# Two fixed places in a step for GpSimd's work on first products, the second behind a wait on VectorE's minimum of pairs

## The chip, the cores and the metric

The kernel runs on one core of a Trainium2 chip. The metric is device time in microseconds (us) of one execution. A core has five engines that run their own queues in order and meet through semaphores: TensorE (PE in the profile, its weight loads PEld), VectorE (DVE), ScalarE (ACT), GpSimd (POOL) and SyncE (SP), which here only starts DMAs.

## The reference

```python
# q, k, v: (8, 8, 576, 64) float32
scores = q @ k^T / 8
kth    = 32nd largest of each row of 576 scores
attn   = softmax(where(scores >= kth, scores, -1e9)) @ v
x      = attn, heads side by side             # (4608, 512)
h      = x @ w_in                             # (4608, 2048)
g      = h if h >= 1; 0 if h <= -1; else (h + 1)^2 / 4
out    = g @ w_out                            # (4608, 512)
```

## The kernel before, in words

**Attention** goes in 144 steps, each for a pair of heads and up to 128 queries. TensorE makes the scores (`sp`, L367), ScalarE scales and copies them to `s` (L368). VectorE finds the 32 largest of each row. It does so on two half-length lists: `more`, the larger of each pair of scores, and `less`, the smaller of each (`pairs`, L381, each a TENSOR_TENSOR with two inputs in SBUF). MAX8 gives eight largest, MATCH_REPLACE8 (L388) takes them out, and so on; a scan (L460) merges the lists into `kth`, and SCALAR_TENSOR_TENSOR (L467, one per head) multiplies the exponentials `e` by `s >= kth` and sums them to `z`. In the next step VectorE takes the reciprocal of `z` (L413), and GpSimd multiplies `e` by it: the *division*, two operations (L420), and a small difference `excess` behind it (L423). ScalarE copies the halves of the words of `e` (L497), and two DMAs bring them turned as `wT`, which TensorE multiplies by `v` (`po`, L514).

**The two products with weights** fill TensorE between these. Four steps complete one tile `xT` of 128 rows. `hidden` (L547) makes the first products of a *group* of two blocks of 128 hidden units, 8 groups per tile; `read` has ScalarE make two relus of it, `r` (L558) and `g` (L566). What is left to do on a group stands in `bound`, on GpSimd: a clip of `r` to 0..1 (L573), its square (L575) and the sum with `g` (L576). `final` (L588) multiplies `g` by `w_out` into `py`, four groups after `hidden`; ScalarE copies `py` to `y` (L594) for the DMA to the output.

**The order** of every engine is the order in which the Python loop calls the operations (`manual_schedule`). The loop goes over steps `m`, each in seven slots. In the part behind the conversion of the weights, slot 0 has VectorE's first operations on step m and the division of step m-1; slot 3 has the maximum of pairs (`more`) of step m+1, the minimum (`less`) of step m and the MAX8 behind them; slot 5 the MAX8 on `less`, the scan and the two products. Slot 2 of every even step has scores for two steps and two `po`, and up to three groups of first products that are read together behind these.

`read` puts its `bound` in the queue `bounds` with the slot's number. At a slot's end those that are more than two slots old are called, three operations together. `read` also empties the queue to one entry first, since `r` has two buffers, and `final` calls entries until its own group is whole. With one tile per four steps, the reads of a cycle come in slots 2 and 5 of its first step, 1 and 5 of the second, 3 of the third, 0, 5 and 6 of the fourth (4 in place of 5 in most cases from step 96 on). "Early", while weights are converted, and behind the last step, the queue is emptied at each slot's end.

Of the kernel before, what the change touches and what calls it, by code (L numbers as in the profile page):

```python
# [11 lines left out]
F32 = mybir.dt.float32  # L12
# [5 lines left out]
ALU = mybir.AluOpType  # L18
# [8 lines left out]
def kernel(  # L27
# [10 lines left out]
    nc = tc.nc  # L38
    B, H, S, D = q.shape
    NTOK, DM = out.shape  # L40
    DFF = moe_w_in.shape[1]
    P = 128
# [8 lines left out]
    SH = S // 2  # L51
# [4 lines left out]
    GROUP = 2  # L56
# [64 lines left out]
    def needed(f, second):  # L121

        return (f // n_in) * (NK + n_in * n_out) + NK + (n_out * (f % n_in + 1) if second else 0)
# [53 lines left out]
    def run(ctx, paired):  # L177
# [197 lines left out]

        def pairs(st, op, name, bufs):
            s = st["s"]
            st[name] = x = att.tile([P, 2, SH], F32, name=name, bufs=bufs)  # L380
            nc.vector.tensor_tensor(out=x, in0=s[:, :, 0:SH], in1=s[:, :, SH:S], op=op)  # L381

        def largest(st, r):
            return [partial(nc.vector.max, out=eight(st["tops"], i, r), in_=st["rest"][:, i, :]) for i in range(2)]
# [6 lines left out]
        def first_top(st, between=None):  # L391
            s, e = st["s"], st["e"]
            if paired:
                pairs(st, ALU.max, "more", 2)
            if between is not None and paired:
                pairs(between, ALU.min, "less", 1)
            st["rest"] = st["more"] if paired else s
            st["tops"] = tops = att.tile([P, 2 * TOP_K], F32, name="tops", bufs=3)
            nmax = att.tile([P, 2], F32, name="nmax")
            for x in largest(st, 0):  # L400
                x()  # L401
            nc.scalar.activation(nmax, tops[:, 0:2 * SPLIT:SPLIT], AF.Copy, scale=-1.0)
            for i in range(2):
                nc.scalar.activation(e[:, i, :], s[:, i, :], AF.Exp, bias=nmax[:, i:i + 1])  # L404
                yield
# [132 lines left out]
        def mlp(xT, rows, pool, last):  # L538
            gs, group, whole_g = {}, 1 if last else GROUP, set()
            py = []  # L540

            def hidden(x):
                ph = ps.tile([P, group, P], F32, name="ph", tag="ph", bufs=3)
                for i in range(group):
                    f = x * group + i
                    for kk in range(NK):
                        nc.tensor.matmul(ph[:, i], w_in[:, kk, f * P:(f + 1) * P], xT[:, kk],  # L547
                                         start=(kk == 0), stop=(kk == NK - 1))

                reads.append(partial(read, x, ph))  # L550
                if not holding:
                    issue_reads()

            def read(x, ph):
                while len(bounds) > 1:
                    bounds.popleft()[1]()
                r = pool.tile([P, GROUP, P], F32, name="r", bufs=2)[:, 0:group]
                nc.scalar.activation(r, ph, AF.Relu, bias=half, scale=0.5 * unit)  # L558
                gs[x] = g = pool.tile([P, GROUP, P], F32, name="g", bufs=2 * LAG)[:, 0:group]
                if last:  # L560
                    nc.scalar.activation(g, ph, AF.Relu, bias=minus_half, scale=0.5 * unit)
                    nc.vector.scalar_tensor_tensor(out=r, in0=r, scalar=1.0, in1=r, op0=ALU.min, op1=ALU.mult)
                    nc.vector.tensor_tensor(out=g, in0=r, in1=g, op=ALU.add)
                    whole_g.add(x)
                    return
                nc.scalar.activation(g, ph, AF.Relu, bias=minus, scale=unit)  # L566
                by_act = converted < n_pieces and x % 2
                if by_act:
                    nc.scalar.activation(r, r, AF.Square)
                bounds.append((slots_done, partial(bound, x, r, g, by_act)))  # L570

            def bound(x, r, g, by_act):
                nc.gpsimd.tensor_scalar(r, r, 1.0, 0.0, ALU.min, ALU.max)  # L573
                if not by_act:
                    nc.gpsimd.tensor_tensor(out=r, in0=r, in1=r, op=ALU.mult)  # L575
                nc.gpsimd.tensor_tensor(out=g, in0=r, in1=g, op=ALU.add)  # L576
                whole_g.add(x)

            def final(f):
                if f == 0:  # L580
                    while outputs:
                        outputs.popleft()[1]()
                    py.append(ps.tile([P, DM], F32, name="py", tag="py", bufs=1))
                if f // group not in gs:
                    issue_reads()
                while f // group not in whole_g:
                    bounds.popleft()[1]()
                nc.tensor.matmul(py[0], gs[f // group][:, f % group], w_out[:, f, :], start=(f == 0), stop=(f == NF - 1))  # L588
                if f == NF - 1:
                    outputs.append((slots_done, partial(give, py[0])))  # L590

            def give(total):
                y = (late or words).tile([P, DM], F32, name="y", bufs=1)
                nc.scalar.activation(y, total, AF.Copy, scale=unit)  # L594
                for p0, p1, dst in rows:
                    nc.sync.dma_start(out=dst, in_=y[p0:p1])

            HALF = DM // 2  # L600

            def final_half(f, c):
                if f == 0:
                    py.append(ps.tile([P, HALF], F32, name="py_half", tag="a" if c else "py", bufs=2 if c else 1))
                nc.tensor.matmul(py[c], gs[f][:, 0], w_out[:, f, c * HALF:(c + 1) * HALF], start=(f == 0), stop=(f == NF - 1))

            def final_halves(f):
                for c in range(2):
                    final_half(f, c)

            def last_finals():
                for c in range(2):
                    for f in range(NF - LAG, NF):
                        final_half(f, c)
                    y = late.tile([P, HALF], F32, name="y_half", tag="y", bufs=1) if c else \
                        pool.tile([P, HALF], F32, name="y_first", tag="r", bufs=2)
                    nc.scalar.activation(y, py[c], AF.Copy, scale=unit)
                    for p0, p1, dst in rows:
                        nc.sync.dma_start(out=dst[:, c * HALF:(c + 1) * HALF], in_=y[p0:p1])

            behind = []
            while pending and pending[-1][3]:
                behind.insert(0, pending.pop())
            for x in range(NF // group + LAG):
                if x < NF // group:
                    pending.append((NK * group, needed(x * group + group - 1, False), partial(hidden, x), False))
                if x < LAG:
                    for _ in range(min(GROUP + 1, len(behind))):
                        pending.append(behind.pop(0)[0:3] + (False,))
                elif last:  # L630
                    if x < NF:
                        pending.append((DM // P, needed(x - LAG, True), partial(final_halves, x - LAG), True))
                    elif x == NF:
                        pending.append((LAG * DM // P, needed(NF - 1, True), partial(last_finals), True))
                else:
                    for f in range((x - LAG) * group, (x - LAG + 1) * group):
                        pending.append((DM // P, needed(f, True), partial(final, f), x >= NF // group))
# [14 lines left out]
        n = len(steps)  # L652
# [8 lines left out]
        converted, inspected, due = 0, 0, 0.0  # L661

        reads, bounds, outputs, holding, slots_done = [], deque(), deque(), False, 0

        def issue_reads():
            while reads:
                reads.pop(0)()
# [118 lines left out]
        for _ in first_top(state[0]):  # L786
            pass
# [18 lines left out]
        for m in range(n + 2):  # L806
            early = converted < n_pieces
# [22 lines left out]
            for slot in range(SLOTS):  # L830
# [66 lines left out]
                slots_done += 1  # L897
                while outputs and (not head or outputs[0][0] < slots_done - 3):
                    outputs.popleft()[1]()
                while bounds and (early or m >= n or bounds[0][0] < slots_done - 2):  # L900
                    bounds.popleft()[1]()
            for _ in (top_k if top_k is not None else ()):
                pass
        while pending:
            advance(32.0, pe_time + 8.0)
            while bounds:
                bounds.popleft()[1]()
            while outputs:
                outputs.popleft()[1]()
        order.__exit__(None, None, None)  # L910
# [14 lines left out]
    with ExitStack() as inner:  # L925
        run(inner, True)
# [31 lines left out]
```

## Time and profile before

| | us |
|---|---|
| Median of 3 runs | 1490.65 (1480.29 to 1490.93) |
| The profiled execution's own time | 1486.83 |
| Its span, first to last instruction | 1485.0 |
| TensorE busy | 1442.5 |
| VectorE busy | 1410.0 |
| ScalarE busy | 1156.4 |
| GpSimd busy | 897.6 |
| GpSimd: clip, square, sum of `bound` | 134.9, 173.0, 280.2 |
| GpSimd: division | 225.9 |
| Mean granted TensorE clock | 0.991 |

How to read it: busy times are unions of intervals in one execution, so two engines can be near the span at once. In a line of groups stand the code line, engine, operation, what it writes and reads, shapes, count, then busy us and mean ns of one, then the engine's idle time just before and what ended it. Timeline lines begin with start and duration in us. Ends of matmuls are modelled; their starts are recorded.

### The profile page before, as it was taken

The numbers are of one execution on the slowest core, as the hardware profiler recorded it, in microseconds if no ns is written. First come the engines' busy times: TensorE is split into PE (matmuls) and PEld (weight loads), VectorE is DVE, ScalarE is ACT, GpSimd is POOL, SyncE is SP. The second block draws the span as 40 slices with busy tenths as digits, with TensorE's granted clock in tenths as the row PEclk, the third lists the DMA queues.
The fourth block names the chain that finished last, engine by engine and source line by source line (L and its number), as shares of the span: only waits on it lengthen the run. The fifth ranks groups of instructions, "written<-read, shape, count | busy, mean of one in ns | idle before, by whom it ended". The sixth has DMA issues, their size and how long they took to land.

```text
span 1485.0 us, 32095 instructions
## 1 busy us (share of the span) xinstructions
PE 1442.5 (97%) x10787; PEld 1053.6 (71%) x10787; DVE 1410.0 (95%) x4391; ACT 1156.4 (78%) x2223; POOL 897.6 (60%) x1310
## 2 busy tenths in 40 slices
PE   7998999999999999999999999999999999999998
PEld 6765677777777777767777777777777777777777
DVE  7988999999999999999999999999999999999922
ACT  7986887877778878888778887888778887787642
POOL 3574366666666666656666656666666666666640
PEclk7999999999999999999999999999999999999999
DMA  8641867875678976887667787887667886665410
GB/s 250 192 118 44 215 177 179 217 183 158 168 176 201 213 202 184 208 226 175 162 168 198 208 205 174 216 215 183 162 178 186 221 206 178 166 164 146 136 41 17
DMA packets 508159, 260.42 MB, mean 175 GB/s; under 512 B 458704, under 2 KB 467152, under 8 KB 507984
## 3 DMA queue, kind: packets, MB, share of 16 engines
q1 hardware_dynamic: 507984, 258.27, 67.7%
q8 instruction: 87, 1.43, 0.4%
q14 instruction: 88, 0.72, 0.2%
HBM read 62.39 MB, written 102.63 MB: 111 GB/s over the span
## 4 chain that ended last, share of the span: by engine, by line
DVE 62%; PE 25%; ACT 5%; issue 5%; DMA 2%; SPq 0%; POOL 0%; ACTq 0%; POOLq 0%; DVEq 0%
DVE more L388 15%; DVE e L467 12%; PE ph L547 8%; PE py L588 8%; DVE less L381 6%; DVE more L381 5%; DVE tops L429 5%; DVE tops L437 5%; DVE tops L448 5%; DVE seconds L455 5%; DVE tops L401 3%; PE sp L367 3%; PE po L514 2%; PE pw L482 1%; DMA wT<-rows 1%
## 5 line engine op out<-in xcount | busy, mean ns | idle before, releaser
L547 PEld LDWEIGHTS ph<-xT,w_in 128*128 128x128 f32 x4608 | 548.4, 192 | 97.0 <-issue 65.5
L547 PE MATMUL ph<-xT,w_in 128*128 128x128 f32 x4608 | 556.7, 276 | 0.6 <-ACT xT L527 0.6
L588 PE MATMUL py<-w_out,g 128*128 128x512 f32 x1120 | 528.3, 599 | 7.2 <-ACT y L594 7.1
L388 DVE MATCH_REPLACE8 more<-tops,more 128x288 f32<-128x288 f32 x864 | 375.1, 437 | 0.0
L573 POOL TENSOR_SCALAR r<-r 128x256 f32<-128x256 f32 x280 | 134.9, 482 | 309.2 <-ACT r L558 305.0
L420 POOL TENSOR_SCALAR e<-e,rz 128x576 f32<-128x576 f32 x268 | 225.9, 853 | 156.1 <-DVE rz L413 156.1
L588 PEld LDWEIGHTS py<-w_out,g 128*128 128x128 f32 x1120 | 193.7, 191 | 173.7 <-issue 172.5
L497 ACT COPY halves<-e 128x1152 uint16<-128x1152 uint16 x268 | 293.4, 1142 | 2.0 <-DMA rows<-halves 2.0
L576 POOL TENSOR_TENSOR g<-r,g 128x256 f32<-128x256 f32 x280 | 280.2, 1001 | 22.0
L467 DVE SCALAR_TENSOR_TENSOR e<-s,kth,e 128x577 f32<-128x577 f32 x288 | 248.8, 899 | 4.4 <-ACT e L404 4.3
L558 ACT ACTIVATE r<-ph,half 128x256 f32<-128x256 f32 (+1 forms) x296 | 136.2, 460 | 136.8 <-PE ph L547 114.0
L404 ACT ACTIVATE e<-s,nmax 128x576 f32<-128x576 f32 x288 | 222.3, 772 | 4.7
L368 ACT ACTIVATE s<-sp 128x576 f32<-128x576 f32 x288 | 171.7, 650 | 27.0 <-PE sp L367 24.8
L575 POOL TENSOR_TENSOR r<-r 128x256 f32<-128x256 f32 x276 | 173.0, 627 | 23.0
L367 PE MATMUL sp<-kT,qT 64*128 64x288 f32 x1024 | 162.5, 435 | 3.7 <-ACT s L368 1.5
L514 PE MATMUL po<-wT,v_in 128*64 128x128 f32 x2048 | 139.1, 276 | 5.5 <-DMA wT<-rows 4.4
L367 PEld LDWEIGHTS sp<-kT,qT 64*128 64x128 f32 x1024 | 90.1, 189 | 73.7 <-issue 33.6
L514 PEld LDWEIGHTS po<-wT,v_in 128*64 128x64 f32 x2048 | 113.6, 137 | 30.3 <-issue 9.0
L566 ACT ACTIVATE g<-ph,minus 128x256 f32<-128x256 f32 x280 | 130.2, 465 | 0.0
L381 DVE TENSOR_TENSOR less<-s 128x576 f32<-128x576 f32 x144 | 129.8, 902 | 0.0
L429 DVE MAX8 tops<-more 128x8 f32<-128x288 f32 x288 | 125.4, 443 | 0.0
L381 DVE TENSOR_TENSOR more<-s 128x576 f32<-128x576 f32 x144 | 117.8, 818 | 5.2 <-ACT s L368 5.1
(95 smaller groups left out, 1378.6 us busy)
## 6 DMA issues: line engine op xcount, KB each, us to landing
rows<-halves SPq DMA_DIRECT2D x134, 576.0 KB, 3.3
lines<-parts SPq DMA_DIRECT2D x48, 256.0 KB, 3.2
q_in<-in_q_dram SPq DMA_DIRECT2D x32, 256.0 KB, 4.2
v_in<-in_v_dram SPq DMA_DIRECT2D x32, 256.0 KB, 3.8
raw<-in_moe_w_in_dram SPq DMA_DIRECT2D x32, 256.0 KB, 3.3
raw<-in_moe_w_out_dram SPq DMA_DIRECT2D x32, 256.0 KB, 3.2
out_dram<-y SPq DMA_DIRECT2D x31, 256.0 KB, 4.7
kT<-in_moe_w_in_dram SPq DMA_DIRECT2D x8, 512.0 KB, 4.6
```

What stands on the lines that cost most here:

```text
L367: nc.tensor.matmul(*x, start=True, stop=True)
L381: nc.vector.tensor_tensor(out=x, in0=s[:, :, 0:SH], in1=s[:, :, SH:S], op=op)
L388: nc.vector.match_replace(out=st["rest"][:, i, :], in_to_replace=eight(st["tops"], i, r - 8), in_values=src[:, i, :], imm_value=LOWEST)
L404: nc.scalar.activation(e[:, i, :], s[:, i, :], AF.Exp, bias=nmax[:, i:i + 1])
L420: nc.gpsimd.tensor_scalar(st["e"][:, i, :], st["e"][:, i, :], rz[:, i:i + 1], 1.0, ALU.mult, ALU.mult)
L429: x()
L467: nc.vector.scalar_tensor_tensor(out=st["all"][1][:, i, :], in0=st["all"][0][:, i, :], scalar=last[i], in1=st["all"][1][:, i, :], op0=ALU. ...
L497: nc.scalar.copy(halves[:, :, i * S:(i + 1) * S], st["e"][:, i, :].bitcast(U16).rearrange("p (k t) -> p t k", t=2))
L514: nc.tensor.matmul(po[j * D:(j + 1) * D], v_in[:, h, c, :] if c < NT else tail_values(v_tl, h, t), wT[:, block(j, c)], start=(c == 0), sto ...
L547: nc.tensor.matmul(ph[:, i], w_in[:, kk, f * P:(f + 1) * P], xT[:, kk], start=(kk == 0), stop=(kk == NK - 1))
L576: nc.gpsimd.tensor_tensor(out=g, in0=r, in1=g, op=ALU.add)
L588: nc.tensor.matmul(py[0], gs[f // group][:, f % group], w_out[:, f, :], start=(f == 0), stop=(f == NF - 1))
```

## The change

`pairs` now returns its instruction, and `first_top` keeps that of the minimum as `pairs_done`. A read no longer queues one function but a list of single operations (clip, square, sum). At the end of slot 0 two operations are called, at the end of slot 3 four, the first of these four with a semaphore wait on the minimum of this step. Before a read the queue is cut to two groups, where one was left before; `r` has three buffers where it had two. Early, and behind the last step, the queue is emptied as before.

```diff
+        pairs_done = None
+
         def pairs(st, op, name, bufs):
...
-            nc.vector.tensor_tensor(out=x, in0=s[:, :, 0:SH], in1=s[:, :, SH:S], op=op)
+            return nc.vector.tensor_tensor(out=x, in0=s[:, :, 0:SH], in1=s[:, :, SH:S], op=op)
...
-                pairs(between, ALU.min, "less", 1)
+                nonlocal pairs_done
+                pairs_done = pairs(between, ALU.min, "less", 1)
...
             def read(x, ph):
-                while len(bounds) > 1:
-                    bounds.popleft()[1]()
-                r = pool.tile([P, GROUP, P], F32, name="r", bufs=2)[:, 0:group]
+                while len(bounds) > 2:
+                    bound_some(len(bounds[0]))
+                r = pool.tile([P, GROUP, P], F32, name="r", bufs=3)[:, 0:group]
...
-                bounds.append((slots_done, partial(bound, x, r, g, by_act)))
-
-            def bound(x, r, g, by_act):
-                nc.gpsimd.tensor_scalar(r, r, 1.0, 0.0, ALU.min, ALU.max)
+                work = [partial(nc.gpsimd.tensor_scalar, r, r, 1.0, 0.0, ALU.min, ALU.max)]
                 if not by_act:
-                    nc.gpsimd.tensor_tensor(out=r, in0=r, in1=r, op=ALU.mult)
-                nc.gpsimd.tensor_tensor(out=g, in0=r, in1=g, op=ALU.add)
-                whole_g.add(x)
+                    work.append(partial(nc.gpsimd.tensor_tensor, out=r, in0=r, in1=r, op=ALU.mult))
+
+                def complete():
+                    whole_g.add(x)
+                    return nc.gpsimd.tensor_tensor(out=g, in0=r, in1=g, op=ALU.add)
+
+                work.append(complete)
+                bounds.append(work)
...
                 while f // group not in whole_g:
-                    bounds.popleft()[1]()
+                    bound_some(1)
...
-                        pool.tile([P, HALF], F32, name="y_first", tag="r", bufs=2)
+                        pool.tile([P, HALF], F32, name="y_first", tag="r", bufs=3)
...
+        def bound_some(amount, behind=None):
+            for _ in range(amount):
+                if not bounds:
+                    break
+                ins = bounds[0].pop(0)()
+                if behind is not None:
+                    tc.add_manual_dep(getattr(ins, "ins", ins), getattr(behind, "ins", behind).name,
+                                      mybir.DependencyInfo(mybir.DependencyClass.Sync, mybir.DependencyReason.ANTI),
+                                      reason="GpSimd's sums stand between VectorE's")
+                    behind = None
+                if not bounds[0]:
+                    bounds.popleft()
...
-                while bounds and (early or m >= n or bounds[0][0] < slots_done - 2):
-                    bounds.popleft()[1]()
+                if early or m >= n:
+                    while bounds:
+                        bound_some(1)
+                elif slot == 0:
+                    bound_some(2)
+                elif slot == 3:
+                    bound_some(4, pairs_done)
...
             while bounds:
-                bounds.popleft()[1]()
+                bound_some(1)
```

## The prediction, made before the change was run

> **What bounds the kernel now.** I read, in this order: busy times and chain of waits, the groups, the timelines of the engines in the middle of the run, and the waits of TensorE.
>
> ```profile
> PE 1442.5 (97%) x10787; PEld 1053.6 (71%) x10787; DVE 1410.0 (95%) x4391; ACT 1156.4 (78%) x2223; POOL 897.6 (60%) x1310
> DVE 62%; PE 25%; ACT 5%; issue 5%; DMA 2%; SPq 0%; POOL 0%; ACTq 0%; POOLq 0%; DVEq 0%
> L467 DVE SCALAR_TENSOR_TENSOR e<-s,kth,e 128x577 f32<-128x577 f32 x288 | 248.8, 899 | 4.4 <-ACT e L404 4.3
> L381 DVE TENSOR_TENSOR less<-s 128x576 f32<-128x576 f32 x144 | 129.8, 902 | 0.0
> L381 DVE TENSOR_TENSOR more<-s 128x576 f32<-128x576 f32 x144 | 117.8, 818 | 5.2 <-ACT s L368 5.1
> ```
>
> Two engines are nearly full. VectorE waits for almost nothing (last column), and between 136 and 1411 us its timeline has no gap: there it sets the pace of the attention steps. One step, from reciprocal to reciprocal, is 9.14 us when every operation is short; 693.33 to 703.23 is 9.90. The reason is in the timelines of that step (start, duration), VectorE first, GpSimd after it:
>
> ```profile
> 693.33 0.14 DVE L413 RECIPROCAL rz<-z 128x2 f32<-128x2 f32 x1
> ...
> 696.17 0.75 DVE L381 TENSOR_TENSOR more<-s 128x576 f32<-128x576 f32 x1
> 696.84 0.75 DVE L381 TENSOR_TENSOR less<-s 128x576 f32<-128x576 f32 x1
> ...
> 700.09 0.38 DVE L460 TENSOR_TENSOR_SCAN kth<-tops,seconds 128x25 f32<-128x25 f32 x1
> ...
> 700.80 0.92 DVE L467 SCALAR_TENSOR_TENSOR e<-s,kth,e 128x577 f32<-128x577 f32 x1
> ...
> 701.65 1.28 DVE L467 SCALAR_TENSOR_TENSOR e<-s,kth,e 128x577 f32<-128x577 f32 x1
> ```
>
> ```profile
> 695.01 0.19 POOL L423 TENSOR_TENSOR excess<-seconds,kth 128x2 f32<-128x2 f32 x1
> 695.17 0.39 POOL L573 TENSOR_SCALAR r<-r 128x256 f32<-128x256 f32 x1
> 695.65 0.61 POOL L575 TENSOR_TENSOR r<-r 128x256 f32<-128x256 f32 x1
> 696.34 1.83 POOL L576 TENSOR_TENSOR g<-r,g 128x256 f32<-128x256 f32 x1
> ...
> 701.18 1.13 POOL L576 TENSOR_TENSOR g<-r,g 128x256 f32<-128x256 f32 x1
> ```
>
> GpSimd's sum at 696.34, 0.73 alone, ran 1.83 because maximum and minimum held it up; the one at 701.18 pushed VectorE's second product from 0.80 to 1.28. Such meetings cost VectorE, by mean less the tenth percentile of all instances in the trace: 144 x (902-743) = 22.9, 144 x (818-740) = 11.2, 288 x (899-805) = 27.1 and the scan 144 x (248-193) = 7.9: together 69 us.
>
> TensorE is the second limit. It repeats every four steps; its mark is the three held groups (48 passes) once per tile of products:
>
> ```profile
> 689.09 5.52 PE L547 MATMUL ph<-xT,w_in 128*128 128x128 f32 x48
> 726.86 5.52 PE L547 MATMUL ph<-xT,w_in 128*128 128x128 f32 x48
> 765.11 5.52 PE L547 MATMUL ph<-xT,w_in 128*128 128x128 f32 x48
> ...
> 1302.56 5.52 PE L547 MATMUL ph<-xT,w_in 128*128 128x128 f32 x48
> 1340.33 5.52 PE L547 MATMUL ph<-xT,w_in 128*128 128x128 f32 x48
> 1378.10 5.52 PE L547 MATMUL ph<-xT,w_in 128*128 128x128 f32 x48
> ```
>
> From 1302 on the marks are 37.77 apart, and there the chain of waits is TensorE alone, without a wait: 37.77 is TensorE's own time for four steps (also met at 689 to 727, where it caught up). Over the whole stage the marks go from 225.95 to 1378.10 in 30 periods: 38.40 each. VectorE's floor is 4 x 9.14 = 36.56.
>
> [...] minimum and maximum, scan and product stretch; MAX8 and MATCH_REPLACE8 (429 to 462 ns in all 2,304 of them) never do. [...] where a GpSimd operation overlapped the start of the maximum by 0.1 us (705.56 + 0.61 against 706.07) the maximum still took 0.75, so I let 0.1 of overlap cost nothing. [...] here 97% hides 0.63 us in 38.40, so I use the spacing of marks.
>
> **The change part by part.** Call GpSimd's three operations a (clip), b (square), c (sum). Starts in a row: a to b 0.48, b to c 0.69, c to a 0.69; lengths 0.40, 0.61, 0.73.
>
> *How many go where.* In the stage the reads are called, over four steps, in slots (2, 5), (1, 5), (3), (0, 5, 6): 8 groups, 24 operations. The new places take 2 + 4 per step, also 24. Carried through slot by slot, the queue settles at once: each slot 0 gets a, b, each slot 3 gets c, a, b, c, never over three groups in the queue. Over the whole run only 16 of 840 are pulled out of place by a read or a final product, all at the head or behind step 141. So no rival rests on misplacing.
>
> *Slot 0.* Behind the reciprocal's end (703.37) come division (703.48), excess, a at +1.70, b until +2.80; the maximum starts at +2.70. Overlap 0.1: nothing. One of four steps has little room: the group read in slot 5 of the last step of the cycle ends on ScalarE at 695.01 where a started at 695.17: 0.16 us to spare. Later than that, b meets the maximum. Price 0 to 0.6 per period.
>
> *Slot 3.* The wait is on the minimum. Released 0.11 behind it (reciprocal to division: 703.37 to 703.48), c starts at +0.11, a +0.80, b +1.28, c +1.97 to +2.70. VectorE then does six MAX8 and a replacement, single-input work; its scan starts at +2.51 (708.02 to 710.53). Overlap 0.19: 0.1 us per step, bounds 0 and 0.2. Queued behind the waiting c are three operations and the next division, which needs the reciprocal 5.0 us after the minimum; GpSimd is done at 2.7. The wait costs nobody, and ScalarE's copies behind the division don't move.
>
> *VectorE's sum:* 36.56 + 4 x 0.1 + about 0.5 for the tight slot = 37.5 in four steps, bounds 36.6 and 38.0. That is below 37.77: **TensorE becomes the pace.**
>
> *Who needs the sums.* c now comes later: the fifth group of a tile was whole at 702.31 and will be at 708.02 + 0.84 = 708.9; its first use is at 711.55. Over all tiles of the stage the smallest room is 2.3 us. Nothing.
>
> *Third r buffer.* ScalarE's waits for a free r (16.9 + 4.7 us) should go; behind VectorE's lead, worth nothing by themselves. y_first only changes its buffer count. No DMA and no queue entry of SP moves.
>
> *Where TensorE's 0.63 us goes.* Its recorded waits in the stage are for ScalarE's copy y (6.3 us, 20 times) and for wT (3.6). The copy y stands in ScalarE's queue behind nmax, exponential and halves, which follow VectorE's maxima: with VectorE ahead it is earlier. The waits for wT are DMA latencies at changes of batch; I let half of them stay, about 2 us.
>
> *Sum:* 30 x (38.40 - 37.77) = 19.1, less 2, is 17. Head (to 226) and tail (from 1378) are bound by conversion and by TensorE: 0, bounds 0 and 4 us. Span 1485.0 - 17 = 1468; the profiled run's own time, 1486.83, goes to 1470. The median of the runs, 1490.65, lies 3.8 above it, so I subtract from the median: 1473.5.
>
> **Rivals.** *VectorE keeps the pace (0.27).* As VectorE leads TensorE by more, the tight read is later against it, and a and b meet maximum and minimum again (0.53 each, 1.28 - 0.75), in time those of the other steps (room 2 us and more). With 1.5 us lost per period it is at 38.06, a gain of 10: 1480. For it: the room of 0.16. Against it: losses slow VectorE, which makes the reads timely again, so it should settle at TensorE's 37.77. I put here also that GpSimd's meetings were hidden by something I don't see, gain 0: 1490.
>
> *Sums too late (0.10), slower.* The c behind the minimum has 2.3 us to its product on TensorE. Were it 2.3 us later (a late read in front of it in GpSimd's order), TensorE would stand; every us beyond costs 30 us in 30 periods. Slower by 1% needs a period of 38.40 + 0.5 = 38.90, so 1.1 us of standing over 37.77: c coming 3.4 us later than worked out: 1506. Against it: a TensorE that lags gives itself more room.
>
> **How the numbers follow.** The likeliest, TensorE as pace, 0.63: 1468 to 1479 by itself. About 1% (15 us) is what can be told from no change; 17 is just over, so I count nine tenths of that case (0.57) and 0.04 of VectorE's as faster: 0.61. The rest of both, 0.06 + 0.23, is same: 0.29. Slower is the late sums: 0.10. The range runs from 1463 (all 19, head and tail 4, and some of the runs' own spread, 1480 to 1491) to 1489, which takes in VectorE's case and leaves out the slower one.
>
> **What would show it.** Minimum near 750 on average, product near 820, scan 200 to 350, GpSimd's sum near 730. Marks of TensorE 37.8 apart, TensorE's share of the chain far above 25%, first VectorE waits for s or e. Wrong would be: marks at 38.4 with short VectorE operations; waits of TensorE on GpSimd's g; a mean of maximum above 850.

## The result, and the profile after

The changed kernel takes 1478.66 us (median of 18 runs, 1475.71 to 1482.41), the kernel before 1489.36 (18 runs): ratio 0.9933, interval 0.9922 to 0.9944, so 10.7 us less. Forecast were 17 us less. The forecast gave 0.61 to a gain of more than about 1%; the measured 0.7% lies in the case to which it gave 0.29. The 10.7 us are also nearer to the 10 us of the rival in which VectorE keeps the pace than to the 17 of the main case, so the time alone doesn't say which engine paces the changed kernel.

The busy times and the chain of waits of the changed kernel, and its groups of VectorE's and GpSimd's operations:

```profile
PE 1440.3 (97%) x10787; PEld 1054.8 (71%) x10787; DVE 1399.0 (95%) x4391; ACT 1156.0 (78%) x2223; POOL 806.3 (54%) x1310
PE 86%; ACT 4%; DMA 4%; DVE 3%; issue 2%; POOL 1%; SPq 1%; ACTq 0%; POOLq 0%; DVEq 0%
```

```profile
L470 DVE SCALAR_TENSOR_TENSOR e<-s,kth,e 128x577 f32<-128x577 f32 x288 | 255.5, 922 | 4.4 <-ACT e L407 4.3
L579 POOL TENSOR_TENSOR g<-r,g 128x256 f32<-128x256 f32 x280 | 225.4, 805 | 110.1 <-DVE less L383 55.5 <-ACT g L569 20.8 <-DVE tops L404 5.3
L383 DVE TENSOR_TENSOR less<-s 128x576 f32<-128x576 f32 x144 | 109.5, 761 | 0.0
L383 DVE TENSOR_TENSOR more<-s 128x576 f32<-128x576 f32 x144 | 109.3, 759 | 5.3 <-ACT s L368 5.3
L463 DVE TENSOR_TENSOR_SCAN kth<-tops,seconds 128x25 f32<-128x25 f32 x144 | 46.0, 319 | 0.0
```

The chain has gone from VectorE (62%) to TensorE (86%). The minimum fell from 902 to 761 ns and the maximum from 818 to 759, but the product *rose* from 899 to 922 and the scan from 248 to 319. VectorE has 11 us less to do, not 69, and its timeline still has no gap in the stage. Read by itself, that looks like an engine that still sets the pace. TensorE's marks say otherwise (its timeline, start and duration):

```profile
651.33 5.52 PE L550 MATMUL ph<-xT,w_in 128*128 128x128 f32 x48
689.11 5.52 PE L550 MATMUL ph<-xT,w_in 128*128 128x128 f32 x48
726.88 5.52 PE L550 MATMUL ph<-xT,w_in 128*128 128x128 f32 x48
764.65 5.52 PE L550 MATMUL ph<-xT,w_in 128*128 128x128 f32 x48
```

Counted from the start of one tile to the start of the next, over the 30 cycles (120 steps, the stage) between the fourth tile and the 34th, 16 cycles take 37.77, the free distance of TensorE, and four take 37.70; in the kernel before it was five and one. So VectorE slowed itself down to TensorE's pace. How it does so is in one step of each timeline, GpSimd first:

```profile
729.25 0.20 POOL L426 TENSOR_TENSOR excess<-seconds,kth 128x2 f32<-128x2 f32 x1
732.13 0.40 POOL L674 TENSOR_SCALAR r<-r 128x256 f32<-128x256 f32 x1 [2.69 <-ACT r L561]
732.61 0.61 POOL L674 TENSOR_TENSOR r<-r 128x256 f32<-128x256 f32 x1
733.30 0.73 POOL L579 TENSOR_TENSOR g<-r,g 128x256 f32<-128x256 f32 x1
...
735.18 1.12 POOL L579 TENSOR_TENSOR g<-r,g 128x256 f32<-128x256 f32 x1
```

```profile
731.04 0.74 DVE L383 TENSOR_TENSOR less<-s 128x576 f32<-128x576 f32 x1
734.30 0.19 DVE L463 TENSOR_TENSOR_SCAN kth<-tops,seconds 128x25 f32<-128x25 f32 x1
734.82 0.89 DVE L470 SCALAR_TENSOR_TENSOR e<-s,kth,e 128x577 f32<-128x577 f32 x1
...
735.65 1.27 DVE L470 SCALAR_TENSOR_TENSOR e<-s,kth,e 128x577 f32<-128x577 f32 x1
```

GpSimd had to wait 2.69 us for ScalarE's read, which TensorE paces (of ScalarE's 120.6 us of idle time before the reads `r`, 115.8 end with TensorE's `ph`). The pair of slot 0 so came behind the minimum, the four of slot 3 behind that, and the last sum, 1.12 us here and 0.73 in the quiet place, pushed the second product to 1.27, where 153 of all 288 products take 0.80 to 0.82. In 61 of the 120 steps of the stage all or part of the pair of slot 0 starts behind the minimum, as here. That VectorE leads TensorE until the reads are late enough for such pushes to eat its lead is a reading of these steps; e1 and e3 below agree with it.

TensorE's recorded waits in the stage, kernel before and then changed (us in all, times, longest), show what it was rid of:

```profile
PE py L588 <- ACT y L594: 6.3, 20, 0.6
PE po L514 <- DMA wT<-rows: 1.9, 2, 1.6
PE po L522 <- DMA wT<-rows: 1.7, 2, 1.3
PE sp L367 <- ACT s L368: 1.0, 1, 1.0
```

```profile
PE sp L367 <- ACT s L368: 1.9, 2, 1.2
PE po L525 <- ACT s L368: 1.5, 1, 1.5
PE po L517 <- DMA wT<-rows: 1.2, 3, 0.7
PE po L525 <- ACT xT L532: 0.4, 1, 0.4
PE po L525 <- DMA wT<-rows: 0.2, 1, 0.2
```

All 20 waits for ScalarE's copy y are gone; those that come at changes of batch are not (4.6 before, 5.2 after).

The two profiled executions differ by less than the medians, spans 1485.0 and 1480.4. In the one of the changed kernel, TensorE ran at half clock from 185.3 to 188.5 and from 1414.1 to 1417.3 us, while it was busy (the table of stretches; the share of the clock is the third number from the right):

```profile
185.30:188.50 3.20, 3.20 (x17) 3.20 (x16) 3.20 (x10) 3.20 (x7) 1.50 (x2) 0.50 0.97 198
1414.10:1417.30 3.20, 3.20 (x34) 3.20 (x33) 0.00 (x0) 0.27 (x1) 0.00 (x0) 0.50 0.02 5
```

In the second one, 16 matmuls of `po` take 1.94 us (from 1415.58), where 16 at 1410.26 took 1.04. Each stretch costs about 1.6 us (an estimate, half of 3.2), and the kernel before has none between 164 and 1484 us in its profile. Between the start of the fourth tile and that of the 34th neither has one: 1152.6 us before (216.7 to 1369.3), 1142.0 after (220.0 to 1362.0). These 10.6 us are as much as the whole gain of the medians (10.7). Head and tail together are 6.0 us longer in this execution of the changed kernel, of which the two stretches are about 3 by the estimate; the rest is not explained. That head and tail give nothing on the median is inferred from this one pair of executions.

### The profile page after: what moved, and what is told of

Same layout as the page of the kernel before. It is cut to its first block, busy times and chain, and to the rows that moved or that the text cites. A ratio compares the mean times of both kernels' runs of the same rounds, so it can differ in the third digit from the quotient of the medians.

```text
span 1480.4 us, 32269 instructions
## 1 busy us (share of the span) xinstructions
PE 1440.3 (97%) x10787; PEld 1054.8 (71%) x10787; DVE 1399.0 (95%) x4391; ACT 1156.0 (78%) x2223; POOL 806.3 (54%) x1310
## 4 chain that ended last, share of the span: by engine, by line
PE 86%; ACT 4%; DMA 4%; DVE 3%; issue 2%; POOL 1%; SPq 1%; ACTq 0%; POOLq 0%; DVEq 0%
PE ph L550 33%; PE py L593 30%; PE sp L367 10%; PE po L517 9%; DMA wT<-rows 1%; PE pw L485 1%; PE po L525 1%; PE py_half L610 1%; DMA lines<-parts 1%; ACT units L147 1%; DVE more L390 1%; ACT e L407 1%; ACT s L368 1%; ACT wT L488 1%; DVE e L470 1%
## 5 line engine op out<-in xcount | busy, mean ns | idle before, releaser
L423 POOL TENSOR_SCALAR e<-e,rz 128x576 f32<-128x576 f32 x268 | 197.0, 745 | 188.4 <-DVE rz L416 188.3
L579 POOL TENSOR_TENSOR g<-r,g 128x256 f32<-128x256 f32 x280 | 225.4, 805 | 110.1 <-DVE less L383 55.5
L674 POOL TENSOR_SCALAR r<-r 128x256 f32<-128x256 f32 x280 | 123.9, 442 | 273.8 <-ACT r L561 269.5
L470 DVE SCALAR_TENSOR_TENSOR e<-s,kth,e 128x577 f32<-128x577 f32 x288 | 255.5, 922 | 4.4 <-ACT e L407 4.3
L561 ACT ACTIVATE r<-ph,half 128x256 f32<-128x256 f32 (+1 forms) x296 | 136.4, 461 | 120.6 <-PE ph L550 115.8
L674 POOL TENSOR_TENSOR r<-r 128x256 f32<-128x256 f32 x276 | 185.6, 672 | 22.9
L432 DVE MAX8 tops<-more 128x8 f32<-128x288 f32 x288 | 125.3, 442 | 0.0
L404 DVE MAX8 tops<-more 128x8 f32<-128x288 f32 x288 | 116.3, 442 | 0.0
L440 DVE MAX8 tops<-more 128x8 f32<-128x288 f32 x288 | 115.9, 441 | 0.0
```

The lines of the kernel that those rows point to most:

```text
L423: nc.gpsimd.tensor_scalar(st["e"][:, i, :], st["e"][:, i, :], rz[:, i:i + 1], 1.0, ALU.mult, ALU.mult)
L470: nc.vector.scalar_tensor_tensor(out=st["all"][1][:, i, :], in0=st["all"][0][:, i, :], scalar=last[i], in1=st["all"][1][:, i, :], op0=ALU. ...
L579: return nc.gpsimd.tensor_tensor(out=g, in0=r, in1=g, op=ALU.add)
L674: ins = bounds[0].pop(0)()
```

## The experiments

Two theories were on trial: A, TensorE paces the changed kernel and VectorE's losses no longer count; B, VectorE, never idle, still does. C, the third buffer for `r` makes the gain, was a third. Four kernels take work from one engine only.

**Less for TensorE, in the changed kernel (e1) and in the one before (e2).**

```diff
-                nc.tensor.matmul(py[0], gs[f // group][:, f % group], w_out[:, f, :], start=(f == 0), stop=(f == NF - 1))
+                if f != 7:
+                    nc.tensor.matmul(py[0], gs[f // group][:, f % group], w_out[:, f, :], start=(f == 0), stop=(f == NF - 1))
```

> The changed kernel with one of the 16 second products per tile left out on TensorE (block 7 of the hidden units adds nothing to the output; the last tile is whole); all else as in the changed kernel. It takes 0.86 us of TensorE's work out of every four steps. Theory A (TensorE paces the changed kernel at 37.77 us per four steps): the marks of TensorE come 37.1 to 37.5 apart, where VectorE takes over, and the time falls to 1458 to 1470. Theory B (VectorE, which never idles, still paces; 37.77 is chance): marks stay at 37.8, only the tail gains, 1475 to 1478. A also expects VectorE's product to fall from 922 ns on average, since TensorE's reads then come sooner against VectorE.

Measured: 1467.41, ratio to before 0.987 (0.9842 to 0.9899), 11 us less than the changed kernel (10 if each is set against the kernel before of its own session). Its marks:

```profile
679.94 5.52 PE L550 MATMUL ph<-xT,w_in 128*128 128x128 f32 x48
716.86 5.52 PE L550 MATMUL ph<-xT,w_in 128*128 128x128 f32 x48
753.77 5.52 PE L550 MATMUL ph<-xT,w_in 128*128 128x128 f32 x48
```

36.91 apart, just 0.86 less. In such cycles VectorE didn't take over, where A had expected 37.1 to 37.5, and its product fell to 846 ns: it gave back losses as A says. Fifteen of the 30 cycles stayed longer (mean of all 37.66), hence 11 us and not 26. TensorE's recorded waits for wT and `s` in the stage are 13.2 us here, 5.2 in the changed kernel, and in this execution two stretches at half clock lie in the stage (591.4 to 598.1 and 1195.6 to 1198.8 us), about 5 us by the same estimate.

> The kernel before with the same second product per tile left out. Both theories have VectorE as the pace of the kernel before, so the marks stay at 38.2 to 38.4 in undisturbed cycles and the time falls only by the tail and by changes of batch: 1482 to 1488. Were the kernel before TensorE's already, it would fall to about 1462.

Measured: 1485.73, ratio 0.998 (0.9966 to 0.9995): about 2.6 us. The time is as expected, the single cycles are not: they take 36.84 to 40.72 us, six of them 36.84 to 36.92, and only their mean, 38.28, stays at VectorE's pace. VectorE's share of the chain is 64%. The same work that was worth 11 us in the changed kernel is worth next to nothing in the one before.

**Less for VectorE, in the changed kernel (e3) and in the one before (e4).**

```diff
+                c = slice(0, SH + 1) if i == 0 else slice(0, S + 1)
-                nc.vector.scalar_tensor_tensor(out=st["all"][1][:, i, :], in0=st["all"][0][:, i, :], scalar=last[i],
-                                               in1=st["all"][1][:, i, :], op0=ALU.is_ge, op1=ALU.mult,
+                nc.vector.scalar_tensor_tensor(out=st["all"][1][:, i, c], in0=st["all"][0][:, i, c], scalar=last[i],
+                                               in1=st["all"][1][:, i, c], op0=ALU.is_ge, op1=ALU.mult,
                                                accum_out=z[:, i:i + 1])
```

> The changed kernel with VectorE's product of the first head of each pair done on half of its row (289 of 577 elements; the other half of those weights stays unmasked). It takes 0.3 us per step off VectorE, 1.2 in four steps. Theory A: the time stays within 3 us of the changed kernel's 1478.7, marks at 37.77; what VectorE gains it gives back in meetings with GpSimd or, at last, in waits. Theory B: 1.2 x 31 = 37 us faster, about 1442.

Measured: 1476.45, ratio 0.993 (0.9903 to 0.9956): the changed kernel's ratio, where B had 1442. Now VectorE waits, as this line of its waits shows:

```profile
DVE e L471 <- ACT e L407: 40.8, 51, 4.4
```

> The kernel before with the same half product left out on VectorE, GpSimd's order untouched. Theory A: VectorE's 38.40 would fall to 37.2, below TensorE's 37.77, so the time meets the changed kernel's: 1476 to 1482, with marks at 37.77 and waits of 38.2 and more only at changes of batch. Theory B, VectorE as the only pace: about 1452.

Measured: 1477.05, ratio 0.9926 (0.9898 to 0.9955). Without touching GpSimd's order, 0.3 us less per step on VectorE gives the same gain as the change. TensorE now has most of the chain, and 18 of 30 cycles take 37.77:

```profile
PE 85%; ACT 6%; DMA 5%; issue 2%; SPq 1%; DVE 0%; POOL 0%; ACTq 0%; POOLq 0%
```

B is out: both ways end at the same wall.

**The wait alone (e5).**

```diff
-                    bound_some(4, pairs_done)
+                    bound_some(4)
```

> The changed kernel without the wait on the minimum: the four operations of slot 3 stand in the same place of GpSimd's order but start when their data is there. If the wait is what keeps the sums off maximum and minimum, the sum behind slot 0's pair meets them again, about one push of 0.53 us per step: VectorE 36.6 + 2.1 = 38.7 or more in four steps, and the time goes back to that of the kernel before, 1486 to 1492. If the places alone do it (the sum blocked by maximum and minimum together, as seen once in the kernel before, costs VectorE nothing), it stays within 3 us of 1478.7.

Measured: 1502.59, ratio 1.0104 (1.0084 to 1.0125): 24 us slower than with the wait, and slower than before. GpSimd and VectorE in one step of it:

```profile
735.60 0.61 POOL L674 TENSOR_TENSOR r<-r 128x256 f32<-128x256 f32 x1
736.29 1.16 POOL L579 TENSOR_TENSOR g<-r,g 128x256 f32<-128x256 f32 x1
```

```profile
736.12 0.74 DVE L383 TENSOR_TENSOR more<-s 128x576 f32<-128x576 f32 x1
736.78 1.28 DVE L383 TENSOR_TENSOR less<-s 128x576 f32<-128x576 f32 x1
```

The sum goes on at once behind the square, starts in the maximum, and gets in between it and the minimum, nearly every time: the minimum is 1217 ns on average. A step is then 9.14 + 0.53 = 9.67 and four are 38.70; 11 of its 30 cycles take 38.64 to 38.72, and the mean of all is 38.67. So the expected cycle was right, and the expected time (to 1492) too short: 38.7 in place of 38.4 in each of 30 cycles is 9 us more than before by itself (7.5 in the traces). As much again lies behind the stage. The cycle that starts with the 34th tile takes 45.58 us, 39.72 in the kernel before and in the changed one. TensorE is at half clock from 1415.6 to 1418.8 us in it, and it waits for GpSimd's sum:

```profile
PE py L593 <- POOL g L579: 3.9, 1, 3.9
```

**The buffer and the queue's length alone (e6), and undone (e8).**

```diff
-                while len(bounds) > 1:
+                while len(bounds) > 2:
...
-                r = pool.tile([P, GROUP, P], F32, name="r", bufs=2)[:, 0:group]
+                r = pool.tile([P, GROUP, P], F32, name="r", bufs=3)[:, 0:group]
```

> The kernel before with three r buffers and the queue cut to two groups at a read, nothing else of the change. Theory A: ScalarE's waits for a free r (21.6 us) are not on the path, same time as before within 3 us. Theory C (the third buffer makes the gain): 1479.

> The changed kernel with two r buffers and the queue cut to one group at a read, as before the change; places and wait stay. By the queue's count one sum in four steps is then pulled out of its place, to the end of slot 2. Theory A: at most one push of 0.53 us in four steps, inside VectorE's slack of about 1 us: 1477 to 1482. Theory C (the third buffer makes the gain): 1486 or more.

Measured: 1488.35 for the part alone, ratio 1.0003 (0.9992 to 1.0014); 1479.18 with it undone, ratio 0.9953 (0.9923 to 0.9983). C is out. In the one profiled execution of e6 (1485.36, its fastest) 15 cycles take 37.77 too, and the stage is 6.9 us shorter than in the profile of the kernel before; the median of 12 executions is that of the kernel before, so nothing is built on that.

**All six operations behind the minimum (e7).**

```diff
-                elif slot == 0:
-                    bound_some(2)
                 elif slot == 3:
-                    bound_some(4, pairs_done)
+                    bound_some(6, pairs_done)
```

> The changed kernel with all six operations behind the minimum and none behind the division. They take 2 x 1.86 = 3.7 us plus 0.1, the scan comes 2.5 us and the products 2.8 us behind the minimum: two of six meet scan and product in every step, at 0.5 us each. If place is what counts, VectorE has 36.6 + 4 x 0.8 = 39.8 in four steps, and the time is above that of the kernel before by some 20 to 45 us. If VectorE's meetings cost nothing now because TensorE paces, it stays at 1479.

Measured: 1495.08, ratio 1.0049 (1.0033 to 1.0066): slower than before, but by 7 us, not 20 to 45. One product in each step:

```profile
744.20 0.40 POOL L674 TENSOR_SCALAR r<-r 128x256 f32<-128x256 f32 x1 [2.54 <-DVE less L383]
...
747.27 1.19 POOL L579 TENSOR_TENSOR g<-r,g 128x256 f32<-128x256 f32 x1
```

```profile
747.07 0.81 DVE L470 SCALAR_TENSOR_TENSOR e<-s,kth,e 128x577 f32<-128x577 f32 x1
...
747.80 1.28 DVE L470 SCALAR_TENSOR_TENSOR e<-s,kth,e 128x577 f32<-128x577 f32 x1
```

Only the last sum is in the way, and it pushes the second product by 0.47: 9.61 per step, 38.44 in four. The scan stayed at 209 ns on average and the first product at 0.81, since the clip ended before it (746.07 + 0.41 against 746.54) and the square overlapped the first product's start by 0.12 only (746.56 + 0.63 against 747.07). My price counted two pushes.

The 7 us over the kernel before are not of the stage: in the traces its 30 cycles take 1151.9 us, 1152.6 in the kernel before. One push in each step costs as much as the mixture of meetings before, and 10 us more than the changed kernel's 1142.0. What is longer than in the kernel before is the cycle that starts with the 34th tile, 46.58 us against 39.72. TensorE is at half clock from 1406.3 to 1413.0 us in it, about 3.4 us by the estimate for such stretches, and it waits for `g`:

```profile
PE py L593 <- POOL g L579: 3.4, 2, 3.1
```

## Why the prediction was right, and where it was too high

- **VectorE paced the kernel before, through meetings with GpSimd.** Shown: less for TensorE was worth 2.6 us (e2), 0.3 us less per step for VectorE 11 (e4).
- **TensorE becomes the pace at 37.77.** Shown by the marks, by 86% of the chain, and by e1 and e3. The number alone fitted the rival as well.
- **The places: two per slot 0, four per slot 3, nothing misplaced.** GpSimd's timeline has this order, but only in 59 of 120 steps do all operations stand on the side of the minimum that they were meant for. The maximum and minimum are nearly free of pushes all the same (759 and 761). The wait lets the sum start 0.17 us behind the minimum, forecast 0.11, and the scan takes 0.33 in quiet steps, 0.13 more, forecast 0.1.
- **The wait costs nobody.** It is worth 24 us (e5). In the changed kernel no matmul has a recorded wait for `g`, so the late sums, the slower rival, did not come; in e5 and e7 they did, in the one cycle behind the stage.
- **The tight read.** Forecast at up to 0.6 us in four steps, as if one step of four had it; 61 of 120 steps have it. It became the regulator: pushes moved to the products (922 ns). The mechanism stood under the rival in which VectorE keeps the pace; what I wrote against it there, that losses make the reads timely again so that it settles at 37.77, fits what happened.
- **The third buffer: nothing.** Shown (e6, e8).
- **The waits for y would go.** They did, 6.3 us to none.

The term that was too small is "less 2", what stays lost at changes of batch. The sum held all of 38.40 against a floor of 37.77 for each of 30 cycles. In the trace after, ten cycles are above 37.77 (with four at 37.70), and their excess is 8.9 us. Of it 5.2 are the recorded waits above, for wT's DMA and for ScalarE's copies of scores and x. About 2.5 are more work on TensorE, an estimate: three cycles have transposes of queries (0.44 over 37.77 in the two of them without a wait), four have the tiles made of row ends (0.30 in the one without a wait). What is left comes with the waits, since a recorded wait tells only part of its cost here: in the kernel before, cycles whose only wait is one for y take about 0.24 us more than that wait adds (a wait of 0.23 goes with 0.47 over 37.77, one of 0.40 with 0.64). The excess is no debt of VectorE's: where VectorE had time to spare it was 8.0 (e3) and 9.0 (e4). So 19.5 of excess before, less 8.9, are the 10.6 measured. I should have taken the floor cycle by cycle: in the trace before, the two cycles behind 257 us take 38.21 each without any wait, which could be read beforehand. So could what the waits for y cost: 6.3 + 20 x 0.24 = 11.1 us, an estimate close to the 10.6 that came.

Three signs that I had named were wrong: first waits of VectorE for s or e (there are none new; pushes took their place), a product near 820 (922), and GpSimd's sum near 730 (805).

What stays open: which of ScalarE's or the DMA queue's entries make TensorE wait at changes of batch. It wasn't tried; by the figures above it is worth no more than about 7 us, an estimate: the excess less the 2.5 of more work. Also open is what puts a single execution on one side: two executions of the kernel before, 1480.29 and 1477.16, were as short as those of the changed kernel, and neither was traced.

## What to carry to other kernels

When two engines are close to each other (here 38.40 and 37.77 us in four steps), removing all of the first one's losses is worth only the distance to the second, and that distance must be measured in every kind of cycle, not in the cleanest one. An engine without a gap in its timeline isn't for that reason the bound: its operations may have stretched to fill the time, so take work away from one engine at a time and see which one the time follows. Where VectorE and GpSimd stretch each other's operations as here, look for those of VectorE that keep their length: in this kernel MAX8 and MATCH_REPLACE8, 429 to 462 ns in all 2,304 instances of either trace. GpSimd's operations at the start of such a stretch, behind a wait, paid here, but no more of them than fit in: the last of six pushed a product by 0.47 us in the step shown (e7). The order alone let the sum slide into the maximum, which cost 24 us (e5).

## What the runs showed of the hardware that was not expected

Whether a sum that starts in the maximum costs VectorE anything changes within some ten nanoseconds of its start (between 169 and 174 ns both outcomes occur). In the kernel before, GpSimd's sum, 0.72 to 0.74 us in 160 of its 280 instances, starts inside the maximum in 78 steps. Where it starts up to about 0.17 us behind the maximum's start (36 steps, 77 to 174 ns), it takes 1.83 to 1.93 us and ends about 0.6 behind the minimum, and VectorE loses nothing: maximum and minimum take 0.74 to 0.76 each. Where it starts from about 0.17 on (42 steps, 169 to 297 ns), it takes 1.12 to 1.16, and the minimum takes 1.27 to 1.29. Without the wait (e5) it starts at 167 ns or later in 126 of 127 such steps, and in all of these the minimum is long; in the one at 163 it is not. The order of the starts does not tell the two outcomes apart: in all 78 steps the sum starts 0.46 to 0.59 us before the minimum, yet in 36 of them the minimum keeps its length. Why is not shown.

The short stretches at half clock (granted share 0.50 in both of the changed kernel's) are the other thing. They lie at different times in different executions (185 and 1414 us in the changed kernel's, 591 and 1195 in e1's, 1406 in e7's); the one at 185 us has TensorE busy for 12.7 of the 15 us before it (170 to 185) and for all of the 15 behind (189 to 204). What starts them is not shown, and that each adds about half its length where TensorE paces stays an estimate.
